# Linear attention and a feed-forward block on one core: seven block products instead of eight in both feed-forward stages, attention run ahead through DRAM, decay tables by scans, weight conversion by integer add

## The chip, the core and the metric

The kernel runs on one core of a Trainium2 chip. The metric is device time in microseconds (us). Before the change the median of three runs is 835.49 us (834.59 to 835.58). TensorE (PE) does the matrix products, VectorE (DVE) and ScalarE (ACT) the elementwise work and the reads of PSUM, GpSimd (POOL) a part of the attention's elementwise work, and SyncE (SP) starts most of the DMA transfers.

## What is computed

A decayed linear attention over 4 batches, 8 heads, 768 positions and head size 64, in float32, and behind it a feed-forward block on the 3072 tokens of 512 features. The weights arrive as 8-byte floats.

```python
for b in range(nb):                                   # blocks of 64 positions
    intra = (q_b @ k_b.T) * Dmask                     # Dmask[i, j] = lam ** (i - j) for i >= j
    out_b = intra @ v_b + (q_b * lam_pow) @ kv_state
    kv_state = lam ** 64 * kv_state + (k_b * rev_pow).T @ v_b
x = out.transpose(0, 2, 1, 3).reshape(3072, 512)
h = x @ w_in                                          # 512 -> 2048
g = np.maximum(0.01 * h, h)
y = g @ w_out                                         # 2048 -> 512
```

The kernel takes blocks of 128 positions instead of 64, which gives the same result.

## The kernel before

There are 24 attention chunks: 4 batches of 6 blocks of 128 tokens. `step(s)` works on three chunks at once, in three stages. Of chunk s it transposes k and q on PE (`transposed`, L203, with a copy out of PSUM on ACT, L205). Of chunk s-1 it forms the scores `ps` (L237), multiplies them by the table `decay` on DVE (L241), and adds the chunk's `pu` (L258) to the recurrent state (L266, L267). Of chunk s-2 it adds the state's part (L225) and the scores' part (L247) in `po` and copies that to `xT`, the feed-forward's input with features on the partitions (L252). k, q and v come in on SP's queue, three chunks ahead (L122).

The table `decay` holds lam to the power i-j for each of the 8 heads. A row of powers is built on 8 partitions by doubling (L97), written to DRAM 128 times (`toep`, L101), and read back with a slanted stride (L106, L111).

The feed-forward runs on 6 groups of 512 tokens. `up(g, f)` makes 128 of the 2048 hidden features for the 512 tokens: 4 matmuls of 128x128 weights by 512 columns (L276) and a leaky ReLU on ACT into `gT` (L278). `down(g, ms)` makes 128 tokens of output: 16 matmuls of 512 columns (L284), a copy (L287) and a store (L289). In float32 each matmul of the program stands in the profile as two MATMUL instructions, each with its own weight load (LDWEIGHTS, engine PEld).

Each of the 32 weight blocks (512 KB, `load_w`, L135 and L137, three blocks ahead) is turned into float32 by `convert_w`: a pass of ACT (L162) and six of DVE (L163 to L169). With the attention of the first group and the whole feed-forward of group 0 the weights are converted one after the other; the steps of later attention chunks are spread evenly between the units of the feed-forward. What stands on an engine's queue next is decided by the order in which the program is written and, within it, by a scheduler that works from its own estimates when the program is built; at run time each engine follows its list.

Of the kernel before, what the change touches and what calls it, by code (L numbers as in the profile page):

```python
# [25 lines left out]
F32 = mybir.dt.float32  # L27
# [18 lines left out]
def kernel(  # L46
# [11 lines left out]
    P = 128  # L58
# [12 lines left out]
    assert D == 64 and KO == HP and S % C == 0 and NCH % CPG == 0  # L71

    const = ctx.enter_context(tc.tile_pool(name="const", bufs=1))
    ldp = ctx.enter_context(tc.tile_pool(name="ldp", bufs=3))
    at2 = ctx.enter_context(tc.tile_pool(name="at2", bufs=2))
    at3 = ctx.enter_context(tc.tile_pool(name="at3", bufs=3))
    wp = ctx.enter_context(tc.tile_pool(name="wp", bufs=2))
    xp = ctx.enter_context(tc.tile_pool(name="xp", bufs=2))
    gp = ctx.enter_context(tc.tile_pool(name="gp", bufs=1))
    tp = ctx.enter_context(tc.tile_pool(name="tp", bufs=2))  # L80
    PS = bass.MemoryType.PSUM
    pp_t = ctx.enter_context(tc.tile_pool(name="pp_t", bufs=2, space=PS))
    pp_s = ctx.enter_context(tc.tile_pool(name="pp_s", bufs=2, space=PS))
    pp_o = ctx.enter_context(tc.tile_pool(name="pp_o", bufs=1, space=PS))
    pp_f = ctx.enter_context(tc.tile_pool(name="pp_f", bufs=3, space=PS))
# [4 lines left out]
    RW = 2 * C + 4  # L90
    prow = const.tile([H, RW], F32, name="prow")
    nc.vector.memset(prow, 0.0)
    nc.vector.memset(prow[:, C:C + 1], 1.0)
    nc.scalar.dma_start(out=prow[:, C + 1:C + 2], in_=lam.rearrange("(h one) -> h one", one=1))
    m = 1
    while m < C:
        nc.vector.tensor_scalar(prow[:, C + 1 + m:C + 1 + 2 * m], prow[:, C + 1:C + 1 + m], prow[:, C + m:C + m + 1], None,  # L97
                                op0=ALU.mult)
        m *= 2
# [4 lines left out]
    flat = toep[:, :, :]  # L104
    for hi in range(2):
        nc.scalar.dma_start(out=decay[:, hi], in_=bass.AP(flat.tensor, flat.offset + hi * C * RW + C,  # L106
                                                          [[RW - 1, P], [2 * C * RW, HP], [1, C]]))

    pow_q = const.tile([P, HP, C], F32, name="pow_q")
    for hi in range(2):  # L110
        nc.scalar.dma_start(out=pow_q[HALF[hi]], in_=bass.AP(flat.tensor, flat.offset + hi * C * RW + C + 1,  # L111
                                                             [[RW, D], [2 * C * RW, HP], [1, C]]))


    loaded = {}

    def load(c):
        b, s0 = c // NCB, (c % NCB) * C
        t = []
        for src, nm, bufs in ((k, "k", 3), (q, "q", 3), (v, "v", 5)):  # L120
# [5 lines left out]
    w_in_sb = [const.tile([P, KO, P], F32, name=f"w_in{f}") for f in range(FO)]  # L126
    w_out_sb = [const.tile([P, d_model], F32, name=f"w_out{f}") for f in range(FO)]
    w_in_r = moe_w_in.rearrange("(ko ki) n -> ki ko n", ki=P)
    w_raw = {}

    def load_w(n):

        w_raw[n] = wp.tile([P, d_model], I64, name="raw", tag="raw", bufs=3)
        if n < FO:
            nc.sync.dma_start(out=w_raw[n].rearrange("p (ko f) -> p ko f", ko=KO), in_=w_in_r[:, :, n * P:(n + 1) * P])  # L135
        else:
            nc.sync.dma_start(out=w_raw[n], in_=moe_w_out[(n - FO) * P:(n - FO + 1) * P, :])  # L137
# [4 lines left out]
    def convert_w(n):  # L142

        raw = w_raw.pop(n)
        hi = raw.bitcast(F32).rearrange("p (n two) -> p n two", two=2)[:, :, 1]
        hii = raw.bitcast(I32).rearrange("p (n two) -> p n two", two=2)[:, :, 1]
        lo = raw.bitcast(U32).rearrange("p (n two) -> p n two", two=2)[:, :, 0]
        w = w_in_sb[n].rearrange("p ko f -> p (ko f)") if n < FO else w_out_sb[n - FO][:, :]
        wi = w.bitcast(I32)
        t = wp.tile([P, d_model], F32, name="wt", tag="wt", bufs=2)
        t = t[:, :]  # L160
        ti = t.bitcast(I32)
        nc.scalar.activation(out=t, in_=hi, func=AF.Abs)  # L162
        nc.vector.tensor_scalar(t, t, HI_MIN, HI_MAX, op0=ALU.max, op1=ALU.min)  # L163
        nc.vector.tensor_scalar(wi, ti, 0x07FFFFFF, 3, op0=ALU.bitwise_and, op1=ALU.logical_shift_left)
        nc.vector.scalar_tensor_tensor(out=wi, in0=hii, scalar=-0x40000000, in1=wi,  # L165
                                       op0=ALU.bitwise_and, op1=ALU.bitwise_or)
        nc.vector.tensor_scalar(ti, wi, -0x00800000, None, op0=ALU.bitwise_and)  # L167
        nc.vector.scalar_tensor_tensor(out=t, in0=lo, scalar=2.0 ** -52, in1=t, op0=ALU.mult, op1=ALU.mult)  # L168
        nc.vector.tensor_tensor(w, w, t, op=ALU.add)  # L169
        if n + W_AHEAD < 2 * FO:  # L170
            load_w(n + W_AHEAD)

    AHEAD = 3
    W_AHEAD = 3
    load(0)
    load_w(0)
    load(1)
    load_w(1)
    load(2)
    load_w(2)  # L180

    ident = const.tile([P, P], F32, name="ident")
    make_identity(nc, ident)
    pow_k = decay[:, :, :, C - 1].rearrange("p hi hp -> p hp hi")
    lam_c = pow_q[:, :, C - 1]


    NST = 3
    state = [const.tile([P, HP, P], F32, name=f"state{i}") for i in range(NST)]
    for t in state:  # L190
        nc.gpsimd.memset(t, 0.0)


    qT, kT, qsT, kd, sc = {}, {}, {}, {}, {}
    xT = {}
# [4 lines left out]
    def transposed(src, nm, bufs):  # L200
        pt = pp_t.tile([P, HP, C], F32, name="pt", tag="pt")
        for hp in range(HP):
            nc.tensor.transpose(out=pt[:, hp, :], in_=pair(src, hp), identity=ident)  # L203
        t = at3.tile([P, HP, C], F32, name=nm, tag=nm, bufs=bufs)
        nc.scalar.copy(t, pt)  # L205
        return t

    def step(s):
        a, b, c = (x if 0 <= x < NCH else None for x in (s, s - 1, s - 2))

        if a is not None:
            if a + AHEAD < NCH:
                load(a + AHEAD)
            kT[a] = transposed(loaded[a][0], "kT", 2)
            if a % NCB < NCB - 1:
                kd[a] = at2.tile([P, H, D], F32, name="kd", tag="kd")
                nc.gpsimd.tensor_tensor(kd[a].rearrange("p (hp hi) d -> p hp hi d", hi=2),  # L217
                                        loaded[a][0].rearrange("p (hp hi) d -> p hp hi d", hi=2),
                                        _bc(pow_k, 3, D), op=ALU.mult)
        if c is not None:  # L220
            po = pp_o.tile([P, HP, C], F32, name="po", tag="po")
            inter = c % NCB > 0
            if inter:
                for hp in range(HP):
                    nc.tensor.matmul(po[:, hp, :], lhsT=state[(c - 1) % NST][:, hp, :], rhs=qsT[c][:, hp, :],  # L225
                                     start=(hp == 0), stop=False, skip_group_check=True)
        if a is not None:
            qT[a] = transposed(loaded[a][1], "qT", 2)
            if a % NCB:
                qsT[a] = at3.tile([P, HP, C], F32, name="qsT", tag="qsT")  # L230
                nc.gpsimd.tensor_tensor(qsT[a], qT[a], pow_q, op=ALU.mult)  # L231

        if b is not None:
            ps = [pp_s.tile([P, HP, C], F32, name="ps", tag="ps") for _ in range(2)]
            for hp in range(HP):
                for hi in range(2):
                    nc.tensor.matmul(ps[hi][:, hp, :], lhsT=kT[b][HALF[hi], hp, :], rhs=qT[b][HALF[hi], hp, :],  # L237
                                     start=(hp == 0), stop=True, skip_group_check=True)
            sc[b] = at2.tile([P, 2, HP, C], F32, name="sc", tag="sc")
            for hi in range(2):  # L240
                nc.vector.tensor_tensor(sc[b][:, hi], ps[hi], decay[:, hi], op=ALU.mult)  # L241

        if c is not None:
            tv = loaded[c][2]
            for hp in range(HP):
                for hi in range(2):
                    nc.tensor.matmul(po[HALF[hi], hp, :], lhsT=tv[:, 2 * hp + hi, :], rhs=sc[c][:, hi, hp, :],  # L247
                                     start=(not inter and hp == 0), stop=True, skip_group_check=True)
# [105 lines left out]
```

## Time and profile before

| | |
|---|---|
| runs | 834.59, 835.49, 835.58 us |
| the profiled execution | 837.49 us, of which the span from first to last instruction is 835.7 us |
| granted TensorE clock, mean | 0.996 |
| HBM read, written | 36.44 MB, 7.36 MB |
| feed-forward matmul instructions (L276, L284) | 768 and 768, 128x512 each |
| feed-forward, PE busy | 331.7 and 335.6 us |

The profile's first part gives each engine's busy time and its share of the span. Its second part cuts the span in 40 slices of 20.9 us, with the busy share in tenths. The chain of waits is the work that ended last, followed back from the end. The groups give, for one line, engine and shape: the count, the busy time, the mean length of one instruction, and the idle time of the engine just before. Matmuls are pipelined, so the mean length of one (some 592 ns) is more than the distance from one to the next; the distance is read from the chain, where a run of x64 matmuls stands with its whole time.

### The profile page before, as it was taken

How to read it: one execution, taken by the hardware profiler on the slowest of the kernel's cores; microseconds unless marked ns; L12 is line 12 of the kernel's file. 1: busy time of each engine (PE TensorE's matmuls, PEld its weight loads, DVE VectorE, ACT ScalarE, POOL GpSimd, SP SyncE). 2: the span in 40 equal slices, each digit the busy share in tenths (PEclk: the TensorE clock that was granted, in tenths of full speed). 3: DMA queues.
4: the chain of work that ended last, by engine and by line, in shares of the span. 5: the costliest groups of instructions: out<-in, count | busy, mean ns of one | idle time of the engine just before them, and what ended most of it. 6: DMA issues, size and time to landing. Idle time of an engine off the chain costs nothing.

```text
span 835.7 us, 6817 instructions
## 1 busy us (share of the span) xinstructions
PE 783.0 (94%) x2816; PEld 397.5 (48%) x2816; DVE 155.3 (19%) x289; ACT 132.3 (16%) x225; POOL 74.2 (9%) x81
## 2 busy tenths in 40 slices
PE   1188997899999999999999999999999999999998
PEld 1175454354554554554544545545545544444443
DVE  0189899910110010100101001101101000000000
ACT  0133333210121110121110111101111100011000
POOL 1062021110110010101101001101100000000000
PEclk9999999999999999999999999999999999999999
DMA  7878565320110120210102201100000000000000
GB/s 144 168 166 215 152 188 194 121 64 13 50 38 0 38 60 16 51 25 13 38 21 55 51 0 38 38 13 23 16 1 1 0 14 25 13 1 0 13 13 25
DMA packets 91767, 44.24 MB, mean 53 GB/s; under 512 B 75864, under 2 KB 86616, under 8 KB 91736
## 3 DMA queue, kind: packets, MB, share of 16 engines
q1 hardware_dynamic: 85632, 35.66, 16.7%
q10 hardware_dynamic: 6104, 8.14, 3.5%
q8 instruction: 22, 0.36, 0.2%
q14 instruction: 9, 0.07, 0.0%
HBM read 36.44 MB, written 7.36 MB: 52 GB/s over the span
## 4 chain that ended last, share of the span: by engine, by line
PE 85%; DVE 7%; DMA 4%; issue 2%; SPq 1%; ACT 0%; POOL 0%; POOLq 0%; ACTq 0%
PE py L284 38%; PE ph L276 34%; PE ps L237 3%; PE po L247 3%; PE pu L258 2%; DMA k<-in_k_dram 2%; PE pt L203 2%; PE po L225 2%; DVE wt L168 2%; DVE w_out L165 1%; DVE wt L163 1%; DMA decay<-toep 1%; DVE wt L167 1%; SPq L135 1%; SPq L122 1%
## 5 line engine op out<-in xcount | busy, mean ns | idle before, releaser
L284 PE MATMUL py<-w_out,gT 128*128 128x512 f32 x768 | 335.6, 598 | 3.7 <-DVE w_out L169 3.7
L276 PE MATMUL ph<-xT,w_in 128*128 128x512 f32 x768 | 331.7, 592 | 0.0
L284 PEld LDWEIGHTS py<-w_out,gT 128*128 128x128 f32 x768 | 146.2, 192 | 186.0 <-issue 179.2
L276 PEld LDWEIGHTS ph<-xT,w_in 128*128 128x128 f32 x768 | 145.0, 190 | 179.4 <-issue 177.6
L241 DVE TENSOR_TENSOR sc<-ps,decay 128x512 f32<-128x512 f32 x48 | 31.3, 687 | 455.2 <-PE ps L237 454.6
L278 ACT ACTIVATE gT<-ph 128x512 f32<-128x512 f32 x96 | 57.0, 595 | 242.9 <-PE ph L276 242.9
L231 POOL TENSOR_TENSOR qsT<-qT,pow_q 128x512 f32<-128x512 f32 x20 | 25.8, 1290 | 478.3 <-ACT qT L205 459.4
L287 ACT COPY osb<-py 128x512 f32<-128x512 f32 x24 | 14.0, 585 | 311.1 <-PE py L284 311.1
L203 PE MATMUL pt<-ident,q 128*128 128x128 f32 x96 | 16.0, 294 | 31.7 <-ACT qT L205 25.9
L258 PE MATMUL pu<-v,kd 128*128 128x128 f32 x160 | 24.1, 296 | 6.6 <-issue 4.2
L237 PE MATMUL ps<-qT,kT 64*128 64x128 f32 x384 | 30.1, 298 | 0.0
L162 ACT ACTIVATE wt<-raw 128x512 f32<-128x512 f32 x32 | 21.7, 679 | 50.4 <-DVE w_out L169 28.3
L203 PEld LDWEIGHTS pt<-ident,q 128*128 128x128 f32 x96 | 11.9, 150 | 33.2 <-ACT qT L205 26.3
L266 POOL TENSOR_TENSOR state<-state,pow_q 64x256 f32<-64x256 f32 x32 | 25.1, 785 | 24.6 <-DVE state L267 13.9
L237 PEld LDWEIGHTS ps<-qT,kT 64*128 64x128 f32 x384 | 25.0, 198 | 4.6 <-issue 4.2
L217 POOL TENSOR_TENSOR kd<-k,decay 128x512 f32<-128x512 f32 x20 | 21.8, 1091 | 55.3 <-DMA decay<-toep 37.8
L247 PE MATMUL po<-sc,v 128*64 128x128 f32 x384 | 26.3, 279 | 0.0
L258 PEld LDWEIGHTS pu<-v,kd 128*128 128x128 f32 x160 | 20.2, 198 | 10.2 <-issue 7.3
L168 DVE SCALAR_TENSOR_TENSOR wt<-raw,wt 128x512 f32<-128x512 uint32 x32 | 24.6, 770 | 0.4
L203 PE MATMUL pt<-ident,k 128*128 128x128 f32 x96 | 15.8, 292 | 6.7 <-DMA k<-in_k_dram 6.7
L247 PEld LDWEIGHTS po<-sc,v 128*64 128x64 f32 x384 | 20.5, 136 | 3.0 <-issue 0.2
L163 DVE TENSOR_SCALAR wt<-wt 128x512 f32<-128x512 f32 x32 | 15.5, 484 | 33.9 <-ACT wt L162 33.9
(27 smaller groups left out, 195.7 us busy)
## 6 DMA issues: line engine op xcount, KB each, us to landing
raw<-in_moe_w_in_dram SPq DMA_DIRECT2D x16, 512.0 KB, 4.4
raw<-in_moe_w_out_dram SPq DMA_DIRECT2D x16, 512.0 KB, 3.2
k<-in_k_dram SPq DMA_DIRECT2D x24, 256.0 KB, 3.6
q<-in_q_dram SPq DMA_DIRECT2D x24, 256.0 KB, 4.1
v<-in_v_dram SPq DMA_DIRECT2D x24, 256.0 KB, 3.6
out_dram<-osb ACTq DMA_DIRECT2D x24, 256.0 KB, 2.0
toep<-prow ACTq DMA_DIRECT2D x1, 1040.0 KB
decay<-toep ACTq DMA_DIRECT2D x2, 256.0 KB, 7.7
```

Source lines behind the costliest of these rows:

```text
L163: nc.vector.tensor_scalar(t, t, HI_MIN, HI_MAX, op0=ALU.max, op1=ALU.min)
L168: nc.vector.scalar_tensor_tensor(out=t, in0=lo, scalar=2.0 ** -52, in1=t, op0=ALU.mult, op1=ALU.mult)
L203: nc.tensor.transpose(out=pt[:, hp, :], in_=pair(src, hp), identity=ident)
L231: nc.gpsimd.tensor_tensor(qsT[a], qT[a], pow_q, op=ALU.mult)
L237: nc.tensor.matmul(ps[hi][:, hp, :], lhsT=kT[b][HALF[hi], hp, :], rhs=qT[b][HALF[hi], hp, :], start=(hp == 0), stop=True, skip_group_check ...
L241: nc.vector.tensor_tensor(sc[b][:, hi], ps[hi], decay[:, hi], op=ALU.mult)
L247: nc.tensor.matmul(po[HALF[hi], hp, :], lhsT=tv[:, 2 * hp + hi, :], rhs=sc[c][:, hi, hp, :], start=(not inter and hp == 0), stop=True, ski ...
L258: nc.tensor.matmul(pu[:, hp, :], lhsT=pair(kd[b], hp), rhs=pair(loaded[b][2], hp), start=(hp == 0), stop=True, skip_group_check=True)
L266: nc.gpsimd.tensor_tensor(new[z], state[(b - 1) % NST][z], _bc(lam_c[HALF[hi]], 2, D), op=ALU.mult)
L276: nc.tensor.matmul(ph, lhsT=w_in_sb[f][:, ko, :], rhs=xT[g][:, ko, :], start=(ko == 0), stop=(ko == KO - 1))
L278: nc.scalar.activation(out=t, in_=ph, func=AF.Prelu, bias=0.0, scale=1.0, alpha=0.01)
L284: nc.tensor.matmul(py, lhsT=gT[f][:, ms * P:(ms + 1) * P], rhs=w_out_sb[f], start=(f == 0), stop=(f == FO - 1))
```

## The change

The diff replaces most of the kernel. It has five parts.

1. **Groups of 256 tokens, seven products.** The input of a group is a 2x2 block matrix A (two halves of 128 tokens, two halves of the inner dimension), and each weight matrix is a 2x2 block matrix B. The four blocks of A B come from seven products of half-sized blocks with sums and differences of blocks (Strassen's scheme in Winograd's form): P1 to P7 of `product`, each `mm(bank, name, first)`. Three PSUM banks Z, Y and W take turns; ACT copies three partial results out (`tmp`, L363), and DVE adds them to a bank (L372, L383, L387). The sums and differences of the inputs (`combine`, L342 to L345) are on DVE, for x and for the hidden activations. Those of the weights (L220, L223, L226) are made once, behind the conversion.

2. **Shapes.** `up(g, u)`, two units for each group, makes four hidden tiles for each of eight pairs in matmuls of 128 columns (L407). `down(g)` makes the output of 256 tokens in matmuls of 256 columns (L426).

```diff
-    MS = 512
-    CPG = MS // C
-    NG = NCH // CPG
+    NG = NCH // 2
...
+        Z = bank("Z")
+        mm(Z, "P1", True)
+        s1 = tmp(Z)
+        tick(us)
+        Y = bank("Y")
+        mm(Y, "P2", True)
+        nc.vector.tensor_tensor(c11[0], s1, Y, op=ALU.add)
+        c11[1]()
+        tick(us)
+        mm(Z, "P6", False)
+        u2 = tmp(Z)
+        tick(us)
+        W = bank("W")
+        mm(W, "P5", True)
+        p5 = tmp(W)
+        tick(us)
+        mm(Z, "P7", False)
+        nc.vector.tensor_tensor(c22[0], p5, Z, op=ALU.add)
...
+        mm(W, "P3", False)
+        nc.vector.tensor_tensor(c12[0], u2, W, op=ALU.add)
...
+        mm(Z, "P4", False)
+        c21(Z)
...
+            for i in range(UP):
+                w = WI[UP * u + i][:, SI[sb], :].rearrange("p (k f) -> p k f", k=2)
+                for kk in range(2):
+                    nc.tensor.matmul(t[:, i * C:(i + 1) * C], lhsT=w[:, kk, :], rhs=x[:, A[sa], kk, :],
...
+            for p in range(NP):
+                nc.tensor.matmul(t, lhsT=G[g][sa][:, p, :], rhs=WO[p][:, SO[sb], :],
```

3. **Attention ahead, through memory.** `step` works on two chunks instead of three, loads two chunks ahead, multiplies k in place, and ends with a store of its result `xc` to the DRAM tile `xs` (L330, on SP's queue, 256 KB). `load_x(g)` brings a group back (L350, two transfers of 256 KB) and combines it. 23 of the 25 steps stand ahead of the first `down`, and with them all 32 weight blocks:

```diff
+            nc.scalar.copy(out=xc, in_=po.rearrange("p a b -> p (a b)"))
+            nc.sync.dma_start(out=xs[b // 2, b % 2], in_=xc)
...
+    load(0)
+    load_w(0, 2)
+    load(1)
+    load_w(0, 4)
+    attend(7)
+    need(FO // 2)
+    load_x(0)
+    up(0, 0)
+    attend(5)
+    need(FO)
+    up(0, 1)
+    attend(11)
+    load_x(1)
+    need(2 * FO)
+    down(0)
+    for g in range(1, NG):
+        up(g, 0)
+        attend(1)
+        up(g, 1)
+        if g + 1 < NG:
+            load_x(g + 1)
+        down(g)
```

The conversions are spread over the steps and products by `tick`, which lets an estimated time's worth of them in; `need(n)` forces the first n blocks. Raw blocks are read up to 8 ahead into the places that the later tables will take.

4. **Decay by scans.** The toeplitz table in DRAM and its readings go; each head's table is one running product along the free axis, started by the identity matrix:

```diff
-    toep = dram.tile([H, C, RW], F32, name="toep")
-    nc.scalar.dma_start(out=toep, in_=_bc(prow[:, :], 1, C))
...
+            nc.vector.tensor_tensor_scan(decay[:, hi, hp, :], _bc(lam_b[:, 2 * hp + hi], 1, C), ident, 0.0,
+                                         op0=ALU.mult, op1=ALU.add)
```

There are 8 such scans of 128x128 (L108) and 4 for `pow_q` (L113).

5. **Conversion by integer add.** Three of the six DVE passes go, one integer add comes in, and ACT makes a second pass over each block:

```diff
-        nc.vector.tensor_scalar(ti, wi, -0x00800000, None, op0=ALU.bitwise_and)
-        nc.vector.scalar_tensor_tensor(out=t, in0=lo, scalar=2.0 ** -52, in1=t, op0=ALU.mult, op1=ALU.mult)
-        nc.vector.tensor_tensor(w, w, t, op=ALU.add)
...
+            nc.scalar.activation(out=v, in_=two.bitcast(U32)[:, :, 0], func=AF.Copy, bias=0.0, scale=2.0 ** -29)
...
+            nc.vector.tensor_tensor(st["di"], st["di"], st["v"], op=ALU.add)
```

**Order on PE, a feed-forward stage.** Before, the rows of PE's list in `up` (numbers behind a name are buffers) read:

```order
L276 MATMUL ph<-xT,w_in_120 128x512 x4
L276 MATMUL ph<-xT,w_in_121 128x512 x4
L276 MATMUL ph<-xT,w_in_122 128x512 x4
L276 MATMUL ph<-xT,w_in_123 128x512 x4
L276 MATMUL ph<-xT,w_in_124 128x512 x4
```

In the change the end of `up(1, 1)` and the start of `down(1)` read (gA_2015 is the block A11 of the hidden activations):

```order
L407 MATMUL W<-x,wi_115 128x128 x2
L407 MATMUL Z<-x,wi_112 128x128 x2
L407 MATMUL Z<-x,wi_113 128x128 x2
L407 MATMUL Z<-x,wi_114 128x128 x2
L407 MATMUL Z<-x,wi_115 128x128 x2
L426 MATMUL Z<-wo_1070,gA_2015 128x256
L426 MATMUL Z<-wo_1141,gA_2015 128x256
```

Each matmul now has 128 or 256 columns instead of 512, with weights of its own, and nothing stands between the two stages.

**Order on PE, the last steps ahead of down(0).** In the change the list reads here (wo_1889 is the last pair of w_out's blocks to be converted):

```order
L270 MATMUL pt<-ident,q 128x128 x3
L310 MATMUL pu<-v,k 128x128 x3
L426 MATMUL Z<-wo_1889,gA_605 128x256
L426 MATMUL Y<-wo_1889,gA_606 128x256
L310 MATMUL pu<-v,k 128x128
L426 MATMUL Z<-wo_1070,gS_610 128x256
L426 MATMUL Z<-wo_1141,gS_610 128x256
```

The scheduler has put P1, P2 and P5 of `down(0)` for the seven other pairs among the attention steps; behind the last pair stand the rest of P1, P2 and P5, the whole of P6, P7, P3 and P4, and then the groups 1 to 11.

**Order on DVE, the start.** Before, the list of DVE starts with the doubling of the row of powers, and goes on to the first block's conversion (t is `wt`):

```order
L97 TENSOR_SCALAR prow<-prow 8x64
L163 TENSOR_SCALAR wt<-wt 128x512
L164 TENSOR_SCALAR w_in_112<-wt 128x512
L165 SCALAR_TENSOR_TENSOR w_in_112<-raw,w_in_112 128x512
L241 TENSOR_TENSOR sc<-ps,decay 128x512 x2
```

In the change it starts so (the scans are listed as SCALAR_TENSOR_TENSOR, the integer add as ISA, on 16-bit halves):

```order
L113 SCALAR_TENSOR_TENSOR pow_q<-lam_p,zero 128x128 x4
L108 SCALAR_TENSOR_TENSOR decay<-lam_b,ident 128x128 x8
L196 TENSOR_SCALAR wi_108<-wi_108 128x2x256
L199 TENSOR_SCALAR wi_108<-wi_108 128x2x256
L202 SCALAR_TENSOR_TENSOR wi_108<-ws,wi_108 128x2x256
L206 ISA wi_108<-wi_108,lo 128x2x512
```

The scans stand ahead of everything else, and each block takes three passes and the add.

More of the change, by code (lines that the diff above doesn't have):

```diff
@@ L91 @@
[L91 to L99, printed above, removed]
-    toep = dram.tile([H, C, RW], F32, name="toep")
-    nc.scalar.dma_start(out=toep, in_=_bc(prow[:, :], 1, C))
+    lam_b = const.tile([P, H], F32, name="lam_b")
@@ L109 @@
     pow_q = const.tile([P, HP, C], F32, name="pow_q")
[L110 to L115, printed above, removed]
+    for hp in range(HP):
+        nc.vector.tensor_tensor_scan(pow_q[:, hp, :], _bc(lam_p[:, hp], 1, C), _bc(zero[:, 0], 1, C), 1.0,
+                                     op0=ALU.mult, op1=ALU.add)
@@ new lines, with load_w, stage_of @@
+    room = [f"wo{i}" for i in range(2, NP)] + ["os", "os"]
+    stage_at = room * 3 + ["wo6", "wo7", "os", "os", "wo7", "os", "os", "os"]
+    w_raw = {}
+    def load_w(done, ahead):
+        while len(w_raw) < min(ahead, 2 * FO - done) and stage_of(len(w_raw) + done, done):
+            load_block(len(w_raw) + done)
+    def stage_of(n, done):
+        before = [m for m in range(n) if stage_at[m] == stage_at[n]]
+        keep = 2 if stage_at[n] == "os" else 1
+        return len(before) < keep or before[-keep] < done
@@ new lines, with tick, need @@
+    queue = [(w, fn, n) for n in range(2 * FO) for w, fn in conversion(n)]
+    credit = 0.0
+    def tick(us):
+        nonlocal credit
+        credit += us * W_RATE
+        while queue and credit > 0:
+            w, fn, _ = queue.pop(0)
+            fn()
+            credit -= w
+    def need(blocks):
+        nonlocal credit
+        while queue and queue[0][2] < blocks:
+            queue.pop(0)[1]()
+            credit = 0.0
+    xs = dram.tile([NG, 2, P, KO * C], F32, name="xs")
+    loaded, qT, kT, qsT = {}, {}, {}, {}
@@ L124, in load @@
         loaded[c] = t
[L126 to L137, printed above, removed]
@@ L173 @@
[L173 to L195, printed above, removed]
@@ L208, in step @@
     def step(s):
[L209 to L231, printed above, removed]
+        a, b = (x if 0 <= x < NCH else None for x in (s, s - 1))
+        inter = b is not None and b % NCB > 0
         if b is not None:
-            ps = [pp_s.tile([P, HP, C], F32, name="ps", tag="ps") for _ in range(2)]
+            ps = [pp.tile([P, HP, C], F32, name="ps", tag="ps", bufs=2) for _ in range(2)]
             for hp in range(HP):
@@ new lines, in step @@
+            po = pp.tile([P, HP, C], F32, name="po", tag="po")
+        tick(1.0)
+        if a is not None:
+            load(a + 2)
+            kT[a] = transposed(loaded[a][0], "kT")
+            if a % NCB < NCB - 1:
+                kr = loaded[a][0].rearrange("p (hp hi) d -> p hp hi d", hi=2)
+                nc.gpsimd.tensor_tensor(kr, kr, _bc(pow_k, 3, D), op=ALU.mult)
+        if inter:
+            for hp in range(HP):
+                nc.tensor.matmul(po[:, hp, :], lhsT=state[(b - 1) % 2][:, hp, :], rhs=qsT[b][:, hp, :],
+                                 start=(hp == 0), stop=False, skip_group_check=True)
@@ new lines, in load_x, with product, bank, tmp @@
+    def load_x(g):
+        x = xp.tile([P, 7, 2, C], F32, name="x", tag="x")
+        for h in range(2):
+            nc.sync.dma_start(out=x[:, 2 * h:2 * h + 2].rearrange("p a k c -> p (a k c)"), in_=xs[g, h])
+        combine(nc.vector, lambda s: x[:, A[s]].rearrange("p k c -> p (k c)"))
+        X[g] = x
+    def product(cols, mm, c11, c12, c21, c22, us):
+        def bank(tag):
+            t = pp.tile([P, 2 * QB], F32, name=tag, tag=tag, bufs=2 if tag == "Z" else 1)
+            return t[:, 0:cols]
+        def tmp(src):
+            t = tp.tile([P, 2 * QB], F32, name="tmp", tag="tmp", bufs=4)
+            nc.scalar.copy(t[:, 0:cols], src)
+            return t[:, 0:cols]
+        Z = bank("Z")
[16 more added lines that the diff above has]
+        nc.vector.tensor_tensor(c22[0], p5, Z, op=ALU.add)
+        c22[1]()
+        tick(us)
+        mm(W, "P3", False)
+        nc.vector.tensor_tensor(c12[0], u2, W, op=ALU.add)
+        c12[1]()
+        tick(us)
+        mm(Z, "P4", False)
+        c21(Z)
+        tick(us)
@@ new lines, in down, with mm, store, quarter @@
+    def down(g):
+        osb = tp.tile([P, 2 * d_model], F32, name="os", tag="os")
+        def mm(t, name, first):
+            sa, sb = PROD[name]
+            for p in range(NP):
+                nc.tensor.matmul(t, lhsT=G[g][sa][:, p, :], rhs=WO[p][:, SO[sb], :],
+                                 start=(first and p == 0), stop=(p == NP - 1), skip_group_check=True)
+        def store(h):
+            m0 = (2 * g + h) * C
+            nc.sync.dma_start(out=out[m0:m0 + C, :], in_=osb[:, h * d_model:(h + 1) * d_model])
+        def quarter(i, then):
+            return osb[:, i * HD:(i + 1) * HD], then
+        def last(z):
+            nc.scalar.copy(osb[:, 2 * HD:3 * HD], z)
+            store(1)
+        product(HD, mm, quarter(0, lambda: None), quarter(1, lambda: store(0)), last, quarter(3, lambda: None), 3.45)
@@ L291, with attend @@
+    W_RATE = 0.7
     at = 0
[L293 removed]
+    def attend(n):
         nonlocal at
[L295 to L323 removed]
+        for _ in range(n):
+            if at <= NCH:
+                step(at)
+                at += 1
```

238 lines of the change are left out of this document (139 added, 99 removed).

## The prediction

> **What bounds the kernel now.** First the page's head: the busy time of each engine, then the slices of PE, DVE, the granted clock and DMA.
>
> ```profile
> PE 783.0 (94%) x2816; PEld 397.5 (48%) x2816; DVE 155.3 (19%) x289; ACT 132.3 (16%) x225; POOL 74.2 (9%) x81
> PE   1188997899999999999999999999999999999998
> DVE  0189899910110010100101001101101000000000
> PEclk9999999999999999999999999999999999999999
> DMA  7878565320110120210102201100000000000000
> ```
>
> PE is full from slice 8 (168 us) to the end. Ahead of that DVE is full and PE is not. So there are two stages: a front stage, in which weights are converted, and a dense stage, in which only PE counts. The chain of waits gives the prices of the dense stage, as whole runs of matmuls:
>
> ```profile
> 182.45 1.09 PE pu L258 x8
> ...
> 215.98 27.47 PE ph L276 x64
> ...
> 307.87 0.89 PE po L225 x8
> ```
>
> 512 columns take 27.47/64 = 0.429 us an instruction, 128 columns in the po run 0.89/8 = 0.111 us. Then the front stage, by windows (start:end, PE, PEld, DVE, ACT, POOL busy with counts, clock, DMA share, GB/s):
>
> ```profile
> 0.00:168.00 168.00, 119.29 (x576) 69.72 (x577) 123.74 (x231) 44.70 (x74) 34.05 (x37) 0.98 0.66 168
> 42.00:168.00 126.00, 112.47 (x544) 64.66 (x544) 118.92 (x217) 40.04 (x67) 30.45 (x27) 0.97 0.61 172
> 30.00:60.00 30.00, 18.33 (x148) 15.70 (x148) 17.97 (x29) 7.58 (x13) 13.20 (x14) 1.00 0.90 204
> 15.00:20.00 5.00, 0.00 (x0) 0.00 (x0) 0.00 (x0) 0.00 (x0) 0.00 (x0) 1.00 0.57 81
> ```
>
> From 42 to 168 us DVE is busy 118.92 of 126 us (94%). From 15 to 20 us no engine works and DMA moves 81 GB/s: the wait for the slanted decay table, which the groups show as POOL's 37.8 us:
>
> ```profile
> L217 POOL TENSOR_TENSOR kd<-k,decay 128x512 f32<-128x512 f32 x20 | 21.8, 1091 | 55.3 <-DMA decay<-toep 37.8
> ```
>
> **The dense stage after the change.** Up: 12 groups x 2 units x 7 products x 8 matmuls x 2 instructions = 2688 instructions of 128 columns. At 0.1113 us that is 299.1 us. Before it was 768 x 0.429 = 329.6 us. Down: 12 x 7 x 8 x 2 = 1344 instructions of 256 columns. No row has 256 columns; the ends are 0.111 (128) and 0.429 (512), and I take the straight line between them, 0.217, which gives 291.9 us against 329.6. A group costs 224 x 0.1113 + 112 x 0.217 = 49.2 us. So the eighth product saved is worth 68 us, not the 82 us that an eighth of 659 us would be: a column costs 4% more in a 128-column matmul and 1% more in a 256-column one.
>
> The price of 128 columns is what the forecast hangs on, because each of these matmuls has its own weight load. The loads of the po run:
>
> ```profile
> L225 PEld LDWEIGHTS po<-qsT,state x160: 190/192/192, 50.2 to 692.8; 128*128 128x128 f32 x160
> 307.71 1.06 PE L225 MATMUL po<-qsT,state 128*128 128x128 f32 x8
> 307.60 0.97 PEld L225 LDWEIGHTS po<-qsT,state 128*128 128x128 f32 x8
> ```
>
> One load takes 0.192 us, but eight stand in 0.97 us: (0.97 - 0.19)/7 = 0.111 us from one to the next, the distance of the matmuls themselves. So loads overlap here with matmuls and with one another, over eight in a row; that it lasts over hundreds is inferred. The ends: 0.111, and 0.192 if each load waited for the last.
>
> [...]
>
> What lies beside PE in this stage: for each up unit (12.5 us of PE) ACT makes three copies and four leaky ReLUs, DVE three additions out of PSUM and four combinations.
>
> ```profile
> L278 ACT ACTIVATE gT<-ph 128x512 f32<-128x512 f32 x96 | 57.0, 595 | 242.9 <-PE ph L276 242.9
> L241 DVE TENSOR_TENSOR sc<-ps,decay 128x512 f32<-128x512 f32 x48 | 31.3, 687 | 455.2 <-PE ps L237 454.6
> L169 DVE TENSOR_TENSOR w_in<-w_in,wt 128x512 f32<-128x512 f32 x16 | 12.1, 753 | 0.1
> L267 DVE TENSOR_TENSOR state<-state,pu 64x256 f32<-64x256 f32 x32 | 13.4, 418 | 10.7 <-PE pu L258 10.2
> ```
>
> ACT 7 x 0.595 = 4.2 us, DVE 3 x 0.687 + 4 x 0.753 = 5.1 us: both half idle. The new waits: P6 may write Z only when ACT has copied P1 out, P7 after the copy of P6, P4 after DVE's addition of P7. Each has one whole product between, 16 x 0.111 = 1.78 us in up, against 0.595 or 0.687 us, so I cost them at nothing. `combine` (3.0 us) must end before P6 of the next down; P1 and P2 (16 x 0.217 = 3.5 us each) cover it. `load_x` waits on SP for the unit's last matmul, with only output stores behind it; its four combinations (128x256, 4 x 0.42 = 1.7 us) stand on DVE ahead of down's first addition, whose bank Y isn't needed again for five products. If the cover failed, each join would show as PE idle of some 0.6 us.
>
> **The front stage after the change.** Behind it lies a sum that is certain; its end, T, must be built. T is when the last pair of w_out is converted. First bytes: 32 blocks of 512 KB, 72 loads of 256 KB, 22 stores to `xs`, and two groups read back (4 x 256 KB) are 41,472 KB, 42.5 MB.
>
> ```profile
> raw<-in_moe_w_in_dram SPq DMA_DIRECT2D x16, 512.0 KB, 4.4
> k<-in_k_dram SPq DMA_DIRECT2D x24, 256.0 KB, 3.6
> ```
>
> Between 30 and 60 us DMA moved 204 GB/s at a share of 0.90, so a full DMA makes 227 GB/s: 42.5 MB last 187 us. Second, DVE. A conversion before has six passes; three remain.
>
> ```profile
> L163 DVE TENSOR_SCALAR wt<-wt 128x512 f32<-128x512 f32 x32 | 15.5, 484 | 33.9 <-ACT wt L162 33.9
> L164 DVE TENSOR_SCALAR w_in<-wt 128x512 int32<-128x512 int32 x16 | 8.9, 556 | 0.2
> L164 DVE TENSOR_SCALAR w_out<-wt 128x512 int32<-128x512 int32 x16 | 6.7, 419 | 0.0
> L165 DVE SCALAR_TENSOR_TENSOR w_out<-raw,w_out 128x512 int32<-128x512 int32 x16 | 12.1, 754 | 0.2
> L168 DVE SCALAR_TENSOR_TENSOR wt<-raw,wt 128x512 f32<-128x512 uint32 x32 | 24.6, 770 | 0.4
> ```
>
> The integer add isn't in the trace. It reads 1024 halves: between 0.75 (as one addition of 512 words) and 1.5 us (a half at a time). I take 0.75, L169, which adds the same words. A block: 0.484 + 0.488 + 0.754 + 0.75 = 2.48 us; the weights' combinations for a pair are 0.753 + 2 x 0.42, or 0.80 us a block. So 3.28 us against 3.69 before (which needs L167, 0.45, and L168 too), 105 us for 32. The second ACT pass lies beside it (ACT was busy 40 of 126 us). The scans aren't in the trace either: between 0.2 and 0.7 us each for 128 elements; 0.3 is near the rows of 64 (0.244) and 256 (0.418) elements, 3.6 us in all.
>
> ```profile
> L97 DVE TENSOR_SCALAR prow<-prow 8x64 f32<-8x64 f32 x1 | 0.2, 244 | 0.0
> ```
>
> To that come 46 score products (31.6 us), 40 state updates (16.7), up(0)'s additions and combinations (10.2) and eight combinations of x (3.4): 170 us of DVE ahead of T.
>
> The two limits follow one another. Up to `load_x(0)` the lists hold 17.5 MB of transfers (9 chunks, 16 blocks, 6 stores, one x), but only some 53 us of DVE (the scans, 8 blocks whole and 4 in part, 16 score products, 13 state updates): DMA sets that part, 77 us and 3 for the first landing. The 117 us of DVE that remain run at the 94% of before: 124.5 us. **T = 80 + 124.5 = 205 us.** The wait for `decay` is gone, but the bytes of slices 8 to 30 now come ahead of T. A check from another view, the pace of attention steps with a conversion each:
>
> ```profile
> 44.46 1.23 PE L237 MATMUL ps<-qT,kT 64*128 64x128 f32 x8
> ...
> 72.82 1.16 PE L237 MATMUL ps<-qT,kT 64*128 64x128 f32 x16
> ```
>
> Four steps in 28.4 us, 7.1 each; 23 steps, 163 us, two up units of 12.5, some 8 at the start and 6 for the last conversions give 202.
>
> **The sum.** Behind T, PE has 70 instructions of down(0) (15.2 us), 11 groups at 49.2 less one product done early (540 us), and the rest of the last two steps (4 us). The end after the last matmul is as before: 831.7 to 835.7, 4 us.
>
> ```profile
> 831.75 0.59 ACT L287 COPY osb<-py 128x512 f32<-128x512 f32 x1 [13.15 <-PE py L284]
> ```
>
> 205 + 15 + 540 + 4 + 4 = 768 us of span, and 1.8 us around it (837.49 against 835.7): **770 us** against the profiled execution's 837.5. The median of the runs shown is 2 us lower than that execution; I leave this in the range.
>
> **Rivals.** (a) The front stage is longer: lists made by estimates put PE's products and DVE's conversions in one order, SP's `xs` store waits for ACT with the next loads behind it, and DMA keeps its mean of before, 168 GB/s: 42.5 MB take 253 us, the end is 818. Slow scans and adds (5 + 24 us) lead there too. For it: idle windows like 15:20; against: that one belongs to the table that goes.
>
> (b) The clock. Two windows show it:
>
> ```profile
> 55.00:60.00 5.00, 1.80 (x16) 1.52 (x14) 4.87 (x9) 0.59 (x1) 2.01 (x3) 1.00 0.81 212
> 140.00:145.00 5.00, 2.63 (x10) 1.70 (x11) 4.97 (x9) 2.11 (x4) 2.10 (x2) 0.83 0.72 198
> ```
>
> PE half idle mostly kept the clock; over 42 to 168 us it was 0.97. PE has some 144 us of work ahead of T (24 steps, up(0), the early part of down(0)); at half clock this would pass T and end at about 850, but at 0.97 it costs 4 us that DVE covers. [...] Counted within (a).
>
> (c) The joins show: 4 writes that wait for a reader in each of 36 sets of products (two up units and a down for each of 12 groups), 0.2 to 0.6 us each, 29 to 86 us: 799 to 856. Against: the cover above.
>
> (d) Slower: the weight loads set the pace of up. Each 0.01 us over 0.111 costs 27 us; the gain of 67 us is gone at 0.136, and 0.192 gives 770 + 217 = 987. For it: the pu run, 1.09/8 = 0.136, just there (its first load isn't hidden). Against: the po run, 20 times the same.
>
> **Chances.** Forecast 0.62, (a) 0.17, (c) 0.10, (d) 0.11. The range reaches from T = 187 (DMA alone), which gives 752, down to 750 for the median's lower level, to the end of (a), 820, and holds the low end of (c). That fewer products are done than said is no rival: the lists hold 1344 and 672 matmuls. Faster by over 0.2%, which is about what a measurement of this kernel can tell from no change: 0.87; within it 0.02; slower 0.11.
>
> **What would show it.** In the profile of the change: runs of L407 x16 at 1.78 us and of L426 x16 at 3.5 us in the chain (step by step 0.111 and 0.217); PE idle only ahead of some 205 us; DVE at 90% or more between 80 and 205 us; the adds of L206 near 0.75 us; first scores ahead of 15 us. Wrong would be: L407 at 0.13 or more, idle PE behind `tmp` or L372 in every group, or a front stage over 225 us.

## The result and the profile after

The change takes 774.62 us in the median (773.65 to 775.64, four runs) against 835.54 us for the kernel before on the same chip: a ratio of 0.927, 95% interval 0.926 to 0.929, 61 us less. The forecast was 770 us, range 750 to 820.

The head of the page of the change, with the same lines as before:

```profile
PE 729.7 (94%) x5312; PEld 672.6 (87%) x5312; DVE 299.8 (39%) x530; ACT 198.4 (26%) x353; POOL 73.2 (9%) x81
PE   4587999888999999999999999999999999999998
DVE  6965799986613223023141230412303223032130
PEclk9889999999999999999999999999999999999999
DMA  9979795976400001000000000000000000000000
```

A slice is now 19.3 us. PE works from the first slice on, and its row holds 9 from the eleventh slice on, the one in which 210 us lies. DVE and DMA are busy for the first eleven slices, which is the front stage. PE is busy 53 us less than before. Its idle time is 773.9 - 729.7 = 44 us, against 53 us before.

The dense stage, in the chain of waits of the change (start, length, what): one group from one `down` to the next, and one product of each kind.

```profile
303.62 3.46 PE Z L426 x16
...
331.37 1.79 PE Z L407 x16
...
352.81 3.46 PE Z L426 x16
```

From the first `down` to the next it is 352.81 - 303.62 = 49.19 us. An instruction of 128 columns takes 1.79/16 = 0.112 us, one of 256 columns 3.46/16 = 0.216 us. The groups show what stands beside that:

```profile
L407 PE MATMUL Z<-x,wi 128*128 128x128 f32 x1536 | 186.7, 275 | 1.0 <-ACT tmp L363 1.0
L407 PEld LDWEIGHTS Z<-x,wi 128*128 128x128 f32 x1536 | 179.5, 192 | 2.4 <-ACT tmp L363 1.2
L426 PE MATMUL Z<-wo,gA 128*128 128x256 f32 x384 | 88.0, 380 | 0.0
```

There are 1536 weight loads of 0.192 us that take 179.5 us in all, 0.117 each: they overlap one another over the whole kernel. PE's idle time ahead of the matmuls of the first row is 1.0 us in all, and it is 0.0 in the rows of the other banks, so the joins are covered.

The front stage by windows (PE, PEld, DVE, ACT, POOL busy, clock, DMA share, GB/s):

```profile
0.00:80.00 80.00, 52.85 (x456) 44.31 (x457) 52.39 (x104) 27.05 (x46) 26.14 (x36) 0.91 0.94 231
80.00:160.00 80.00, 72.62 (x668) 65.34 (x667) 75.63 (x133) 42.44 (x74) 28.32 (x27) 1.00 0.80 204
160.00:210.00 50.00, 44.17 (x387) 38.04 (x386) 34.13 (x56) 16.63 (x30) 17.53 (x19) 0.97 0.64 160
```

DMA is full for the first 80 us (0.94, 231 GB/s). Then DVE is (75.63 of 80 us). From 160 to 210 us nothing is full: DVE 68%, DMA 0.64, PE 88%. The end of the stage, T, stands in the timeline: the last raw block is asked for at 199.23 us, behind a store of `xs` on SP, and its first matmul runs at 209.80 us.

```profile
198.80 0.34 SPq L330 DMA_DIRECT2D xs<-xc  x1
199.23 0.38 SPq L160 DMA_DIRECT2D os<-in_moe_w_out_dram  x1
...
206.48 0.68 ACT L192 ACTIVATE wo<-os 128x512 f32<-128x512 f32 x1
...
209.80 0.70 PE L426 MATMUL Z<-wo,gA 128*128 128x256 f32 x2
```

### The profile page after: what moved, and what is told of

It is laid out like the page before. It is cut to its first block, busy times and chain, and to the rows that moved or that the text cites. A ratio compares the mean times of both kernels' runs of the same rounds, so it can differ in the third digit from the quotient of the medians.

```text
span 773.9 us, 12415 instructions
## 1 busy us (share of the span) xinstructions
PE 729.7 (94%) x5312; PEld 672.6 (87%) x5312; DVE 299.8 (39%) x530; ACT 198.4 (26%) x353; POOL 73.2 (9%) x81
## 4 chain that ended last, share of the span: by engine, by line
PE 83%; DVE 10%; issue 3%; ACT 2%; POOL 1%; DMA 1%; SPq 0%; ACTq 0%; DVEq 0%; POOLq 0%
PE Z L426 21%; PE Z L407 20%; PE W L426 11%; PE W L407 10%; PE Y L426 5%; PE Y L407 5%; PE ps L283 3%; PE pt L270 2%; PE po L326 2%; PE pu L310 2%; PE po L299 2%; DVE sc L287 1%; DVE wo L202 1%; DVE wo L206 1%; DVE state L319 1%
## 5 line engine op out<-in xcount | busy, mean ns | idle before, releaser
L407 PE MATMUL Z<-x,wi 128*128 128x128 f32 x1536 | 186.7, 275 | 1.0 <-ACT tmp L363 1.0
L407 PEld LDWEIGHTS Z<-x,wi 128*128 128x128 f32 x1536 | 179.5, 192 | 2.4 <-ACT tmp L363 1.2
L407 PE MATMUL W<-x,wi 128*128 128x128 f32 x768 | 93.9, 275 | 0.0
L407 PEld LDWEIGHTS W<-x,wi 128*128 128x128 f32 x768 | 89.8, 192 | 0.0
L426 PE MATMUL Z<-wo,gA 128*128 128x256 f32 x384 | 88.0, 380 | 0.0
L426 PE MATMUL W<-wo,gS 128*128 128x256 f32 x384 | 87.2, 379 | 0.0
L426 PE MATMUL Z<-wo,gS 128*128 128x256 f32 x384 | 86.9, 379 | 0.0
L426 PEld LDWEIGHTS W<-wo,gS 128*128 128x128 f32 x384 | 72.9, 190 | 10.0 <-issue 0.2
L426 PEld LDWEIGHTS Z<-wo,gS 128*128 128x128 f32 x384 | 72.8, 190 | 9.8
L426 PEld LDWEIGHTS Z<-wo,gA 128*128 128x128 f32 x384 | 71.6, 190 | 9.4 <-DVE wo L206 0.2
L363 ACT COPY tmp<-Z 128x512 f32<-128x512 f32 (+1 forms) x72 | 37.0, 514 | 156.2 <-PE Z L426 108.5
L383 DVE TENSOR_TENSOR gA<-tmp,Z 128x512 f32<-128x512 f32 x24 | 16.5, 687 | 103.2 <-PE Z L407 103.2
L383 DVE TENSOR_TENSOR os<-tmp,Z 128x256 f32<-128x256 f32 x12 | 5.1, 421 | 114.2 <-PE Z L426 114.2
L372 DVE TENSOR_TENSOR gA<-tmp,Y 128x512 f32<-128x512 f32 x24 | 16.5, 688 | 80.3 <-PE Y L407 80.2
L407 PE MATMUL Y<-x,wi 128*128 128x128 f32 x384 | 47.5, 276 | 0.0
L407 PEld LDWEIGHTS Y<-x,wi 128*128 128x128 f32 x384 | 45.2, 192 | 0.4 <-issue 0.2
L426 PE MATMUL Y<-wo,gA 128*128 128x256 f32 x192 | 44.4, 379 | 0.0
L426 PEld LDWEIGHTS Y<-wo,gA 128*128 128x128 f32 x192 | 36.2, 190 | 4.8
L287 DVE TENSOR_TENSOR sc<-ps,decay 128x512 f32<-128x512 f32 x48 | 31.2, 686 | 22.2 <-PE ps L283 11.2
```

Source lines behind the costliest of these rows:

```text
L287: nc.vector.tensor_tensor(sc[:, hi], ps[hi], decay[:, hi], op=ALU.mult)
L363: nc.scalar.copy(t[:, 0:cols], src)
L372: nc.vector.tensor_tensor(c11[0], s1, Y, op=ALU.add)
L383: nc.vector.tensor_tensor(c22[0], p5, Z, op=ALU.add)
L407: nc.tensor.matmul(t[:, i * C:(i + 1) * C], lhsT=w[:, kk, :], rhs=x[:, A[sa], kk, :], start=(first and i == 0 and kk == 0), stop=(i == UP ...
L426: nc.tensor.matmul(t, lhsT=G[g][sa][:, p, :], rhs=WO[p][:, SO[sb], :], start=(first and p == 0), stop=(p == NP - 1), skip_group_check=True)
```

## The experiments

Theory 1 is the forecast's: seven products are worth what PE saves, and the front stage is bound by DMA for 80 us and by DVE behind that. The runs were timed in three groups, in which the kernel before has medians of 836.26 to 836.60 us, up to 1 us more than beside the change itself, so that a difference to the change of 1 us says nothing. Beside each ratio stands its 95% interval.

**Eight products.** P2 is computed twice, so that only the number of products differs.

```diff
         mm(Y, "P2", True)
+        mm(Y, "P2", True)
```

> The change with P2 computed twice (the second pass overwrites the first), so eight products instead of seven, everything else alike. Theory 1, the dense stage is PE alone and the gain is the eighth product: each group gets 2 x 1.79 + 3.45 = 7.0 us more, 12 groups 84 us, so about 859 us, which is slower than the kernel before (835.5). Rival, joins or other engines set the dense stage: less than 84 us, since the extra product fills gaps.

Measured: 857.23 us, ratio 1.024 (1.022 to 1.027). That is 82.6 us more than the change, against 84 expected, and slower than the kernel before. The dense stage is PE alone: the extra product finds next to no gap to fill. With an eighth product, and the sums and differences kept, the change is a loss.

**Scans alone, in the kernel before.** The slanted table through DRAM goes, the scans come in, nothing else.

```diff
-    toep = dram.tile([H, C, RW], F32, name="toep")
...
+            nc.vector.tensor_tensor_scan(decay[:, hi, hp, :], _bc(lam_b[:, 2 * hp + hi], 1, C), ident, 0.0,
+                                         op0=ALU.mult, op1=ALU.add)
```

> The kernel before with only the decay tables by scans. Theory 1, PE's idle time ahead of 42 us (35 us) is the wait for the slanted table: scores can start near 10 us, the conversions too, DMA still has to bring the first chunks: about 22 us less, 813 us. Rival, the front stage of before is set by the conversions alone and only shifts its idle time: within 5 us of 835.

Measured: 803.32 us, ratio 0.961 (0.960 to 0.963): 33 us less, half as much again as expected, and more than half of what the whole change gains. The head of its page:

```profile
PE 784.0 (98%) x2816; PEld 396.8 (50%) x2816; DVE 157.2 (20%) x294; ACT 132.4 (17%) x225; POOL 75.8 (9%) x82
PE   6999979999999999999999999999999999999998
```

PE is busy from the first slice, and idle for 801.6 - 784.0 = 17.6 us instead of 52.7. Not only the wait ahead of 42 us went: PE's idle time fell from 35.2 to 8.3 us ahead of 42 us, and from 13.5 to 5.6 us between 42 and 168 us. A likely reason for the second part, argued and not tried: the feed-forward of group 0, with 512 tokens, gives PE 8 x 0.429 = 3.4 us of work for each weight block, and DVE needs 3.7 us to convert one, so that the two nearly keep step once they start together. The edit takes out the wait for the table and the table's own transfers at once. In the first 42 us DMA moved 223 GB/s, against 156 before. How much of the 33 us is the wait and how much the faster loads was not separated.

**The table through DRAM, put back into the change** (the same edit the other way).

> The change with the decay tables of before (through DRAM) instead of scans. Theory 1, attention cannot start before some 40 us and PE idles there: about 22 us more, 797 us. Rival, the front stage has slack on DVE and PE behind 160 us that takes it up: 5 us more or less, 780 us.

Measured: 797.70 us, ratio 0.954 (0.951 to 0.956): 23 us more, as theory 1 had it, and 10 us less than the scans are worth in the kernel before. In its first window PE does one set of transposes and waits:

```profile
0.00:40.00 40.00, 1.09 (x4) 0.71 (x4) 3.43 (x12) 1.94 (x2) 1.63 (x8) 1.00 0.78 170
```

**The integer add alone, in the kernel before.**

```diff
+        nc.scalar.activation(out=vi, in_=lo, func=AF.Copy, bias=0.0, scale=2.0 ** -29)
...
-        nc.vector.tensor_scalar(ti, wi, -0x00800000, None, op0=ALU.bitwise_and)
-        nc.vector.scalar_tensor_tensor(out=t, in0=lo, scalar=2.0 ** -52, in1=t, op0=ALU.mult, op1=ALU.mult)
-        nc.vector.tensor_tensor(w, w, t, op=ALU.add)
+        nc.vector.tensor_tensor(wi, wi, vi, op=ALU.add)
```

> The kernel before with only the integer-add conversion: 32 x 1.15 = 37 us of DVE less. Theory 1, only PE's idle time counts, and between 42 and 168 us that is 126 - 112.5 = 13.5 us: 8 to 13 us less, about 825 us. Rival, DVE bounds the front stage outright: its end moves by 37 us, 800 us.

Measured: 828.26 us, ratio 0.991 (0.989 to 0.994): 8 us less, the low end of theory 1. DVE did 155.3 - 121.8 = 33.5 us less, and only a quarter of that shortened the kernel.

**Attention spread.** 7 steps ahead of the first `down` instead of 23, two to a group behind it.

```diff
     up(0, 0)
-    attend(5)
     need(FO)
     up(0, 1)
-    attend(11)
     load_x(1)
...
         attend(1)
         up(g, 1)
+        attend(1)
```

> The change with only 7 attention steps ahead of the first down and the others spread two to a group. Theory 1, DVE bounds the front stage from about 80 us on and attention's PE work lies in its gaps: T falls from 210 to about 165 us (16 steps x 2.2 us of DVE at 94%), but 16 steps x 5 us of PE work come into the dense stage: about 774 - 42 + 80 = 812 us. Rival, DMA bounds the front stage throughout: T falls to about 130 us (16.8 MB less ahead of it), so 775 to 785 us.

Measured: 803.57 us, ratio 0.960 (0.957 to 0.963): 29 us more than the change, where theory 1 had 38 and the rival 0 to 10. The first P6, which marks the end of the front stage, starts at 163 us instead of 211 (T was expected at 165 by theory 1, at 130 by the rival), and the windows show where the attention's work was missed:

```profile
80.00:165.00 85.00, 67.58 (x442) 58.05 (x441) 77.32 (x151) 40.05 (x68) 18.24 (x11) 0.88 0.59 164
165.00:802.00 637.00, 618.20 (x4419) 573.03 (x4417) 166.36 (x275) 132.81 (x239) 36.63 (x36) 1.00 0.12 36
```

From 80 to 165 us PE stands still for 17 us and its clock falls to 0.88. Behind 165 us it is idle for 19 us; the steps that now stand between products wait for DVE's score products (L287), 13.4 us in all and 10.3 us of it at `pu` alone. So running these steps ahead is worth 29 us here.

**More and less work for DVE in the front stage.** First each block's clamp is done twice:

```diff
             nc.vector.tensor_scalar(st["d"], st["d"], HI_MIN, HI_MAX, op0=ALU.max, op1=ALU.min)
+            nc.vector.tensor_scalar(st["d"], st["d"], HI_MIN, HI_MAX, op0=ALU.max, op1=ALU.min)
```

> The change with the clamp of each weight block done twice (the second changes nothing): 32 DVE passes of about 0.6 us more. Theory 1, DVE bounds the front stage behind 80 us: some 23 blocks lie there, 23 x 0.6 / 0.94 = 15 us more, about 789 us. Rival, DMA bounds it: 0 to 4 us more.

Measured: 780.91 us, ratio 0.933 (0.930 to 0.936): 6 us more, between the two. Then the clamp and the shift are left out:

> The change without the clamp and the shift of each weight block (two DVE passes left out, so the weights are other numbers): 32 x 1.1 = 35 us less on DVE. Theory 2, the end of the front stage then meets DMA (42.5 MB at 227 GB/s, 190 us) and the attention steps' own pace: 12 to 18 us less, about 760 us. Theory 1, DVE bounds everything behind 80 us: 24 x 1.1 / 0.94 = 28 us less, 746 us.

Measured: 765.17 us, ratio 0.915 (0.913 to 0.917): 9.5 us less, a little short of theory 2 and far from the 28 us of theory 1. The engines' busy times in the one and in the other:

```profile
PE 737.7 (94%) x5312; PEld 678.9 (87%) x5312; DVE 311.4 (40%) x562; ACT 198.5 (25%) x353; POOL 80.1 (10%) x81
PE 724.6 (95%) x5312; PEld 669.0 (88%) x5312; DVE 276.8 (36%) x466; ACT 198.2 (26%) x353; POOL 74.9 (10%) x81
```

The busy time of DVE rose by 11.6 us in the one and fell by 23.0 us in the other, which is 0.36 us a pass and not the 0.6 or 0.55 expected. With these sizes theory 1 gives 23 x 0.36 / 0.94 = 9 us more for the second clamp and 24 x 0.72 / 0.94 = 18 us less without clamp and shift. So the first run alone (6 us, uncertain by 2.5) doesn't speak clearly against it, but the second does, with half of that. A microsecond of DVE moved the end by about half of one. This is where theory 1 falls: DVE does not bound all that lies behind 80 us. Theory 2, formed ahead of the second run, says that DVE is full from 80 to 160 us alone, and that beyond that the steps wait for one another.

**More bytes.** Each attention result is stored a second time, to a DRAM tile that nobody reads.

```diff
             nc.sync.dma_start(out=xs[b // 2, b % 2], in_=xc)
+            nc.sync.dma_start(out=xs2[b // 2, b % 2], in_=xc)
```

> The change with each chunk's attention result stored a second time to a DRAM tile that nobody reads: 24 x 256 KB more on the same queue. Theory 1, DMA bounds only the first 80 us: 6 stores, 1.6 MB, 7 us more, about 781 us. Rival, DMA bounds the whole front stage: 5.8 MB / 227 GB/s = 25 us more, about 800 us. If DMA has room everywhere: within 2 us of 774.6.

Measured: 775.61 us, ratio 0.927 (0.925 to 0.929): no difference that can be told. DMA bounds neither the whole front stage nor, by the stores at least, its first 80 us: there DMA moved 247 GB/s instead of 231.

**Four tries to shorten the front stage.** The stores of `xs` on ACT's queue instead of SP's:

```diff
-            nc.sync.dma_start(out=xs[b // 2, b % 2], in_=xc)
+            nc.scalar.dma_start(out=xs[b // 2, b % 2], in_=xc)
```

> The change with the stores of the attention results started by ACT, right behind the copy that makes them, instead of by SP, where the next loads wait behind them. Theory 1, the last weight blocks came late (issued at 199 us behind such a wait): 3 to 8 us less, about 769 us. Rival, SP's order is not on the path: within 2 us of 774.6, or a little slower for ACT's time (24 x 0.35 us).

Measured: 779.90 us, ratio 0.933 (0.931 to 0.935): 5 us slower, outside both. The sums of the weight blocks on POOL (the three operations of L220, L223 and L226 on the other engine):

> The change with the sums and differences of the weight blocks on POOL instead of DVE: 25 us less on DVE, some 35 us more on POOL, all ahead of 210 us. Theory 2, DVE is full only between 80 and 160 us, and behind that the attention steps themselves set the pace (7 us each): 5 to 8 us less, about 768 us. Rival, POOL's own part of each step (k, q and state, 4 us) is on that path: 5 us more, 780 us. Theory 1, DVE bounds everything behind 80 us: 18/0.94 = 19 us less, 756 us.

Measured: 788.92 us, ratio 0.943 (0.936 to 0.949): 14 us slower, so neither theory; the rival was right, and its size is nearly three times what I gave it. On POOL the sum of 128x512 takes twice as long as on DVE, as the groups of this run and then of the change show:

```profile
L220 POOL TENSOR_TENSOR wi<-wi 128x512 f32<-128x512 f32 x8 | 13.3, 1658 | 15.2 <-DVE wi L206 15.1
```

```profile
L220 DVE TENSOR_TENSOR wi<-wi 128x512 f32<-128x512 f32 x8 | 6.5, 818 | 0.1
```

POOL was busy 125.6 us instead of 73.2, and DVE from 80 to 160 us only 66 us. The rate at which conversions are let in, 0.85 instead of 0.7:

> The change with the conversions let in at a rate of 0.85 instead of 0.7 for each estimated us: more conversion early, less behind 160 us. Theory 2, idle DVE behind 160 us and idle PE ahead of 80 us stay: within 4 us of 774.6. Rival, the mix of conversions and steps is what leaves DVE idle behind 160 us, and the end of the front stage moves by 8 us: 766 us.

Measured: 782.13 us, ratio 0.936 (0.934 to 0.939): 7.5 us slower, outside what either theory gave. Five raw blocks ahead instead of eight for the first six conversions:

```diff
-            load_w(n + 1, len(room))
+            load_w(n + 1, 5 if n < 6 else len(room))
```

> The change with only 5 raw weight blocks instead of 8 asked for ahead while the first 6 are converted, so that chunks 3 and 4 of the attention come in 1.5 MB (7 us) earlier. Theory 2, PE idles 27 us ahead of 80 us because the bytes come in the wrong order: PE's idle time there falls by some 7 us and the clock stays up, 5 us less, 769 us. Rival, the sum of bytes ahead of 80 us is what counts: within 2 us of 774.6.

Measured: 773.66 us, ratio 0.926 (0.923 to 0.928), the same as the change, where theory 2 had 5 us less. PE's idle time ahead of 80 us fell by 1 us (27.2 to 26.2) and not by 7, so this change in the order of the first bytes doesn't matter. Three of the four are slower, by 5 to 14 us, and none is clearly faster: each changes the lists that the scheduler makes for all engines, and which part of the loss is the edit and which the new lists was not separated.

The traces do show where the loss of two of them is not. With the stores on ACT the first P6 starts at 206.89 us, and at the higher rate at 208.29, 4 and 3 us earlier than in the change (210.99), and still the kernels end later. Their lists leave more for PE behind T. In the first of the two a whole attention step starts at 236.75 us, where the change has none:

```profile
206.89 3.62 PE L426 MATMUL Z<-wo,gS 128*128 128x256 f32 x16
...
236.75 1.16 PE L283 MATMUL ps<-qT,kT 64*128 64x128 f32 x16
```

By 210 us PE had begun 1455 and 1448 matmuls in these runs, against 1505 in the change. An earlier T alone is no gain.

## Why the prediction was right, point by point

**The dense stage.** 128 columns: 0.1113 us forecast, 0.112 measured. 256 columns, from the straight line: 0.217 and 0.216. A group: 49.2 and 49.19 us. The rival that weight loads set the pace is out: 0.192 us a load, and still 0.112 us from one matmul to the next over whole products. The rows of L407 decide it.

**The joins.** Costed at nothing; 1.0 us in all was measured. The cover of one product (1.79 us) was enough for every copy and addition.

**The first 80 us.** Forecast as set by DMA, with 53 us of DVE; measured 52.39 us of DVE, a DMA share of 0.94, and 231 GB/s against the 227 used. The scans took 0.34 and 0.33 us each (0.3 forecast), and scores began at 12.42 us:

```profile
4.24 1.37 DVE L113 TENSOR_TENSOR_SCAN pow_q<-lam_p,zero 128x128 f32<-128x128 f32 x4
5.53 2.61 DVE L108 TENSOR_TENSOR_SCAN decay<-lam_b,ident 128x128 f32<-128x128 f32 x8
12.42 2.08 PE L283 MATMUL ps<-qT,kT 64*128 64x128 f32 x16 [0.68 <-ACT qT L272]
```

That more bytes would move its end is not shown: the second stores cost nothing, and the order of the first loads neither. So DMA was full there, but that it set the length of this part, as the forecast has it, stays open.

**From 80 us to T.** T came at 209.8 us, 205 forecast. But the step behind it, that the remaining 117 us of DVE run at 94%, is right only to 160 us (95%). Behind that DVE is at 68%, and two errors nearly cancelled, which is luck: DVE's busy time was some 8 us less (162.15 us by 210 us, 170 forecast), and DVE stood idle 16 us of the last 50, 20.2 us of the whole part where the forecast has 7.5. The rest behind T came as forecast, 773.9 - 209.8 = 564 us against 563. In the chain of waits from 160 to 210 us nearly half (47%) is PE's attention matmuls, and the runs with more and less DVE work agree: half a microsecond for one. That the remainder behind T is fixed, as the sum takes it, isn't so in general: the two runs with an earlier T and a later end show it. Rival (b) put PE's work ahead of T at 144 us; PE was busy 169.6 us of the 210, at a mean granted clock of 0.96 (0.97 forecast). The integer add was 0.80 and 0.83 us (0.75 forecast).

```profile
L206 DVE CUSTOM_DVE_ANT_0 wo<-wo,lo 128x1024 uint16<-128x1024 uint16 x16 | 13.2, 830 | 0.6
```

**What the sum hid.** The forecast gave the eighth product saved 68 us and took the front stage as one block. The kernel before with scans alone lets it be split, in the spans of the profiled executions. The feed-forward is the number of its instructions times their distance, 1536 x 0.429 = 659 us in the first two columns and 300 + 290 = 590 us in the third; the rest of PE's busy time is mostly attention.

| us | before | before, with scans | the change |
|---|---|---|---|
| feed-forward | 659 | 659 | 590 |
| rest of PE's busy time | 124 | 125 | 140 |
| PE idle | 53 | 18 | 44 |
| span | 835.7 | 801.6 | 773.9 |

Scans take away 35 us of idle time. The other four parts together then save 69 us of PE work, and give back 26 us as idle time and 15 us as more busy time outside the feed-forward, so that 28 remain. A likely reason, argued and not tried by itself: up(0) on 256 tokens gives PE 25 us for 16 weight blocks, 1.6 us each instead of 3.4, and the attention that goes ahead to fill the gap has waits of its own. I had the size of the whole, but had not seen that these parts would lose 41 us again, as idle and busy time of PE in the front stage.

## What to carry to other kernels

Where PE is full, count its instructions at the distance that a run of the same shape has in the chain of waits; the forecast of the dense stage came out of two rows to 0.1%. Where no engine is full, busy sums gave a stage's length only by luck here: look for the stretch in which the bounding engine is idle, and try each part of a change by itself, since here the plainest part, a table made by scans, brought more than half of the gain when it was made alone. A saving in arithmetic that comes with smaller groups can leave PE with less to do in the stage where it waits for weights.

## What the runs showed of the hardware

The granted clock of PE fell in the front stage in a way that can be read. Here is a window and, from the timeline of PE (start, length, what, idle before), the rows behind it:

```profile
30.00:40.00 10.00, 2.78 (x13) 2.04 (x11) 8.93 (x19) 3.04 (x5) 1.06 (x1) 0.67 0.98 236
```

```profile
39.23 1.11 PE L270 MATMUL pt<-ident,q 128*128 128x128 f32 x4 [7.13 <-ACT kT L272]
41.08 2.08 PE L283 MATMUL ps<-qT,kT 64*128 64x128 f32 x16 [0.73 <-ACT qT L272]
43.09 2.07 PE L299 MATMUL po<-qsT,state 128*128 128x128 f32 x8
...
51.10 1.16 PE L299 MATMUL po<-qsT,state 128*128 128x128 f32 x8
```

PE waited 7.13 us for a copy on ACT. In the timeline of ACT, two passes over weight blocks stand ahead of that copy, and wait for DVE's integer adds (L206) of other blocks:

```profile
35.82 0.68 ACT L192 ACTIVATE wi<-ws 128x512 f32<-128x512 f32 x1 [4.57 <-DVE wi L206]
38.03 0.68 ACT L192 ACTIVATE wi<-os 128x512 f32<-128x512 f32 x1 [1.53 <-DVE wi L206]
38.62 0.56 ACT L272 COPY kT<-pt 128x512 f32<-128x512 f32 x1
```

Behind that wait, eight po instructions took 2.07 us, against 1.16 eight microseconds later and 1.06 in the kernel before: about half speed, for some 10 us. PE stopped at 32.1 us, and the granted clock was 0.50 from 35.53 to 45.77 us. The same trace shows it behind a shorter wait too. Here PE had stood still for 2.32 us, and the clock was 0.50 in the window at the wait's end (the second line, a window as above):

```profile
28.85 2.05 PE L310 MATMUL pu<-v,k 128*128 128x128 f32 x8 [2.32 <-issue]
28.70:32.12 3.42, 3.16 (x12) 2.50 (x12) 2.33 (x6) 1.22 (x2) 0.00 (x0) 0.50 0.80 155
```

In the kernel before, the clock fell to 0.50 at 160.37 us behind an idle stretch of 2.77 us. What lowers the clock was not tried by itself.

Such stretches at 0.50 are a part of the 15 us of busy time that came in outside the feed-forward. An estimate, from PE's busy time in windows of 2 us times the share of the clock that was missing in each: 5.9 us of PE's busy time were lost to the clock ahead of 210 us, against 3.2 us ahead of 168 us in the kernel before, so some 3 of the 15. Where the other 12 come from was not measured.
